# An infini-attention and FNet kernel whose planned order gets biases by kind of task and a jitter, drawn anew for each part of the plan

## The chip, the cores and the metric

The kernel runs on one core of one Trainium2 chip, as one program. The metric is the device time of one execution in microseconds. Before the change it is 1710.0 us, the median of three runs (1707.21 to 1713.73). The engines are called as in the profile: PE (TensorE), DVE (VectorE), ACT (ScalarE), POOL (GpSimd) and SP, which issues the DMAs. PEld is PE's loading of weights.

## The reference

Two layers, each of them an attention block with a compressive memory and then a Fourier mixing block, on 2048 rows of 512 numbers. Cut to what is computed:

```python
def A(x, wq, wk, wv, wo, beta):                 # 32 heads of 16, 4 segments of 512 rows
    q, k, v = heads(x @ wq), heads(x @ wk), heads(x @ wv)
    M, z = 0, 0
    for s in range(4):
        p = softmax(qs @ ks.T * scale + mask)   # inside the segment, causal
        a_mem = (phi(qs) @ M) / (phi(qs) @ z + 1e-6)
        o = g * a_mem + (1 - g) * (p @ vs)
        M, z = M + phi(ks).T @ vs, z + sum(phi(ks))
    return concat(o) @ wo

def B(x, seq_re, seq_im, hid_re, hid_im):
    a, b = x @ hid_re.T, x @ hid_im.T
    return seq_re @ a - seq_im @ b

for _ in range(2):
    x = x + A(layernorm(x), ...)
    x = x + B(layernorm(x), ...)
```

## The kernel before

Nearly all products are formed from pairs of float16 tiles: a number is split into a high and a low part, and three matmuls (high by high, high by low, low by high) add into one PSUM bank. Every tile that goes into such a product is therefore made by an ACT copy and a subtraction on DVE or POOL.

The work is cut into 32 attention groups (2 layers, 4 segments, 4 groups of 8 heads; the index `i`) and into Fourier units. Each kind of work is a Python generator in `body`:

- `s_p` and `s_v` project q, k and v (PE names `b<-g,w` and `b<-w,g`: `g` is the transposed layer-norm tile). `t_split` lays q and k out through DRAM into `qst` and `kst`.
- `s_x` multiplies q with k to find each row's maximum (`b<-kst,qst`, 62 rows of the array); `t_max` reduces each bank on DVE into `mx` (the custom instruction that writes `junk`). A transpose of `mx` on PE (`b<-identf,mx`) and a DMA put the maxima into two spare rows of `qst`.
- `s_st` forms the scores again, transposed and with the maximum taken off (`b<-qst,kst`, 64 rows); `t_sel` does exp on ACT and the causal mask on POOL (the affine selects).
- `s_av` multiplies with v (`b<-w,vt`, tiles of 128 by 32, four side by side); `s_m` and `t_merge` merge memory and attention; `s_o` is the output projection (`b<-wo,w`), after which `t_res` and `t_ln` add the residue and normalise.
- `s_c` turns the stored sequence matrix into float16 pairs, four tiles at a time: DVE maxima `cam`, a small matmul over the partitions (`b<-cam,ones`), a chain on DVE that gives the scale `csu`, ACT copies, and a subtraction.
- `s_ab` is the hidden transform of a row tile (`b<-wd,w`); `s_f` the sequence transform (`b<-w,w`, 128x512: 12 matmuls to a unit), each of whose units `t_y` adds into `y` on DVE.
- In the second layer the last two chunks of the sequence transform (`WIN` and up) are done with fewer multiplications: `t_sums` builds sums of matrix tiles on POOL and ACT, `t_six` sums of the hidden transform's results, and `t_win` multiplies them (`b<-w,w`, 128x256, 672 matmuls at the very end of the program).

The array is used in three tile shapes: whole (128 by 128), two halves of rows side by side (`mode="h"`: `s_x`, `s_st` and the read of the memory in `s_mem`), and four quarters of columns (`mode="v"`: `s_av`).

The order of all instructions is set when the program is built. `Plan` keeps a time for each engine, for each tile's last write and read, and for the slots of the shared SBUF and PSUM pools. A generator yields what its next step needs: engine, tiles read, pool slots, and the tile shape. The loop at lines 1391 to 1431 asks `Plan.ready` when each waiting step could start by the plan's clock, takes the larger of that and the time at which the step's engine is free, and then runs the first step in the list among those with the smallest time (lines 1426 and 1427, `SLACK` is 0). `Plan.turn` (line 67) adds `SWITCH`, 95 plan nanoseconds, where a PE step would change the tile shape, except that after `HOLD` = 700 nanoseconds in the whole shape it doesn't. `BESIDE` puts off a quarter step where a whole-shape step could start by then, and `TWICE` puts off the half steps of `s_x` and `s_st` until two of them fit, at most 1000 nanoseconds. Each engine runs its instructions in the order in which the loop wrote them; semaphores hold an instruction until its inputs are there. Every instruction is recorded by one helper (line 260), so all rows of the profile carry L260 and tiles are told apart by name: `w` is any slot of the shared SBUF pool, `b` any PSUM bank.

Of the kernel before, what the change touches and what calls it, by code (L numbers as in the profile page):

```python
# [2 lines left out]

# [29 lines left out]
BF16 = mybir.dt.bfloat16  # L33
NEG = -1e30
TICK = 10240 / 3
SLACK = 0
HOLD, SWITCH = 700.0, 95.0
TWICE, EARLY, BESIDE = 1000.0, 0.0, 1000.0
RESERVE = dict(G=500.0, Y=1000.0, V=0.0, A=0.0)
BATCH = 4  # L40
AGAIN = 0.0
FIRST = "cc", "craw"
NR = 3
K8192 = struct.unpack("<f", b"\x00\x70" * 2)[0]


class Plan:
# [4 lines left out]
    def __init__(self):  # L52
        self.free = dict.fromkeys("VGATYHD", 0.0)
        self.acc = {}
        self.cols = {}
        self.wr = {}
        self.rd = {}
        self.area, self.count, self.slot = {}, {}, {}
        self.fresh = set()
        self.port = dict(V=(0.0, 0.0), G=(0.0, 0.0))  # L60
        self.fine = {}
        self.by = {}
        self.late = False
        self.dma = None
        self.mode, self.units, self.begun, self.entered = "m", {}, 0.0, 0.0

    def turn(self, mode):

        now = self.free["T"]
        if mode == self.mode or self.mode == "m" and now - self.entered >= HOLD:  # L70
            return now
        return max(now, *self.units.values(), 0.0) + SWITCH

# [18 lines left out]
    def slots_free(self, kinds):  # L92
        extra, taken, r = {}, {}, 0.0
        for k in kinds:
# [8 lines left out]
            if n + len(busy) >= cap:  # L103
# [3 lines left out]
            keep = sum(max(0, lo - self.count[o] - extra.get(o, 0)) for o, (lo, _) in ar["kinds"].items()  # L107
                       if o != k and (n >= low or o in FIRST) and not (self.late and k == "ab" and o == "pt"))
            if k in ("ss", "sx") and n >= 4:
# [157 lines left out]
def body(ctx: ExitStack, tc: tile.TileContext, x, wq, wk, wv, wo, beta, wd, cs, out):  # L267
    nc = tc.nc
    pl = Plan()
    V, G, A, T, Y = (Eng(e, k, pl) for e, k in zip(  # L270
        (nc.vector, nc.gpsimd, nc.scalar, nc.tensor, nc.sync), "VGATY"))
# [46 lines left out]
    V.memset(mhalf, -0.5)  # L318
    kst = [const.tile([128, NP, 512], F16, name=f"kst{i}") for i in range(NR)]
    qst = [const.tile([128, NP, 512], F16, name=f"qst{i}") for i in range(NR)]  # L320
    vt = [const.tile([128, TT, NP, 3, 16], F32, name=f"vt{i}") for i in range(NR)]
    identf = const.tile([128, 128], F32, name="identf")
# [13 lines left out]
    def need(eng, *reads, tag=(), mode="m"):  # L336
        return eng, reads, (tag,) if isinstance(tag, str) else tag, mode
# [5 lines left out]
    def gate(*keys):  # L343
        return lambda: all(k in done for k in keys)
# [65 lines left out]
    used = set()  # L410

    def keep(n, g, w):
        yield gate(("dk", 0))
        yield need("Y", w)
        Y.dma_start(wqkv[g][n], w)
        yield lambda: (n, g) in used
        pl.close(w)

    def s_w():
        def part(n, g, how):  # L420
            i = 2 * g + n if n < 2 else 8
            yield need("A", tag="wv" if n == 2 else "wt")
            w = sb("wv" if n == 2 else "wt", F16, (128, 2, KT, 128))
            yield from how(w, stage[g][n], scl[:, i:i + 1])
            wnow[n, g] = w
            done.add(("W", n, g))
            if g < 2 and n < 2:
                spawn(keep(n, g, w))
            else:
                yield need("Y", w)  # L430
                Y.dma_start(wqkv[g][n], w)
# [77 lines left out]
    def s_k():  # L509
# [5 lines left out]

        for i in range(NR):
            for t, c in ((qst[i], 0.0), (kst[i], K8192)):
# [6 lines left out]
            if i == 0:  # L524
# [4 lines left out]
                yield gate(*[("L", 0, t) for t in range(TT)])  # L529
                for j in range(NR):  # L530
                    V.memset(vt[j][:, :, :, 1, :], 1.0)
# [119 lines left out]
    def t_split(p, key, f, kphi):  # L651
# [21 lines left out]
        i = key[1]  # L673
        if i >= NR:
            yield gate(("ST", i - NR))
# [160 lines left out]
    def s_psum():  # L836
        yield gate("WO")
        pl.floor("dft", 1)
        yield gate(("E", 3))
        kinds = pl.area["ss"]["kinds"]  # L840
        kinds["ss"], kinds["sx"] = (2, 6), (0, 6)

# [533 lines left out]
    def t_out(t, k):  # L1376
        yield gate(*[(*k, i) for i in range(6)])
        for i in range(2):
            yield need("Y", y)
            Y.dma_start(fins[1][t + i], y[:, t + i, :])  # L1380

    streams = [[None, s()] for s in (s_r, s_c, s_st, s_ln, s_w, s_x, s_mem, s_v, s_p, s_ab, s_f, s_wo, s_k, s_b, s_psum)]
    hots += [[None, s()] for s in (s_m, s_o, s_av,)]
    for s in hots + streams:
        s[0] = next(s[1])
    def settle(s):
        while callable(s[0]) and s[0]():
            s[0] = next(s[1], None)
        return s[0] is not None and not callable(s[0])

    while streams or hots or tasks or lows:
        best = None
        moved = True
        while moved:
            moved = False
            for s in hots + tasks + streams + lows:
                if callable(s[0]) and s[0]():
                    settle(s)
                    moved = True
        for group in (hots, tasks, lows):  # L1400
            group[:] = [s for s in group if s[0] is not None]
        streams[:] = [s for s in streams if s[0] is not None]
        ready, raw = [], {}
        for s in hots + tasks + streams + lows:
            w = s[0]
            if not callable(w):
                r = pl.ready(w[1], w[2], w[0])
                if r is not None:
                    free = pl.turn(w[3]) if w[0] == "T" else min(pl.free[e] for e in w[0])
                    ready.append((max(r, free), s))  # L1410
                    raw[id(s)] = r
        if pl.mode == "m":
            other = min((r for r, s in ready if s[0][0] == "T" and s[0][3] == "m"), default=1e18)
            for j, (r, s) in enumerate(ready):
                if s[0][0] == "T" and s[0][3] == "v" and r >= other:
                    ready[j] = max(r, raw[id(s)] + BESIDE), s
        if pl.mode != "h":
            other = min((r for r, s in ready if s[0][0] == "T" and s[0][3] != "h"), default=1e18)
            for j, (r, s) in enumerate(ready):
                w = s[0]  # L1420
                if w[2][:2] in (("ss", "ss"), ("sx", "sx")) and r + EARLY >= other:
                    both = pl.ready(w[1], w[2] + w[2][:2], w[0])
                    late = raw[id(s)] + TWICE
                    ready[j] = max(r, late if both is None else min(both, late)), s
        if ready:
            first = min(r for r, _ in ready)
            best = next(q for q in ready if q[0] <= first + SLACK)
        if best is None:
            assert not streams and not tasks, "stuck"
            break  # L1430
        best[1][0] = next(best[1][1], None)
# [45 lines left out]
```

## Time and profile before

| what | before |
|---|---|
| median of 3 runs | 1710.0 us |
| the profiled execution's own time | 1710.03 us |
| its span, first to last instruction | 1708.3 us |
| instructions | 33012 |
| DVE busy | 1174.4 us (69%) |
| ACT busy | 867.9 us (51%) |
| POOL busy | 848.4 us (50%) |
| mean granted TensorE clock | 0.987 |
| bytes moved by DMA | 228.16 MB |

A busy time is the union of an engine's instructions. Matmuls are pipelined, so a matmul's own duration is longer than the distance from its start to the next one's start; the rows of a timeline give both. A row of the view by windows gives, for a stretch of the span, each engine's busy time with its number of instructions, then the granted clock of TensorE, the share of time in which the DMA engines were busy, and GB/s.

### The profile page before, as it was taken

How to read it: one execution, taken by the hardware profiler on the slowest of the kernel's cores; microseconds unless marked ns; L12 is line 12 of the kernel's file. 1: busy time of each engine (PE TensorE's matmuls, PEld its weight loads, DVE VectorE, ACT ScalarE, POOL GpSimd, SP SyncE). 2: the span in 40 equal slices, each digit the busy share in tenths (PEclk: the TensorE clock that was granted, in tenths of full speed). 3: DMA queues.
4: the chain of work that ended last, by engine and by line, in shares of the span. 5: the costliest groups of instructions: out<-in, count | busy, mean ns of one | idle time of the engine just before them, and what ended most of it. 6: DMA issues, size and time to landing. Idle time of an engine off the chain costs nothing.

```text
span 1708.3 us, 33012 instructions
## 1 busy us (share of the span) xinstructions
PE 1640.5 (96%) x11324; PEld 765.1 (45%) x11324; DVE 1174.4 (69%) x3617; ACT 867.9 (51%) x1437; POOL 848.4 (50%) x1304
## 2 busy tenths in 40 slices
PE   5979999999999999999999999999999999999999
PEld 2424434344444443444444444444444443444488
DVE  6886776697968787455587776856777676442266
ACT  5558657628555556534446754454544444530341
POOL 6536647356544654443334654344643442570672
PEclk9979999999999999999999999999999999999999
DMA  8644635444654533344954764344544222416263
GB/s 207 163 137 119 177 106 158 131 124 127 171 148 127 167 106 100 117 111 154 248 150 161 209 171 117 76 114 133 131 109 116 76 75 63 131 25 197 86 185 118
DMA packets 221944, 228.16 MB, mean 134 GB/s; under 512 B 113232, under 2 KB 139856, under 8 KB 221776
## 3 DMA queue, kind: packets, MB, share of 16 engines
q1 hardware_dynamic: 221776, 226.06, 47.0%
q8 instruction: 89, 1.46, 0.4%
q14 instruction: 79, 0.65, 0.1%
HBM read 140.51 MB, written 61.87 MB: 118 GB/s over the span
## 4 chain that ended last, share of the span: by engine, by line
PE 77%; DVE 8%; issue 5%; ACT 4%; POOL 3%; DMA 2%; SPq 1%; ACTq 0%; POOLq 0%; DVEq 0%
PE b L260 77%; ACT w L260 4%; DVE junk L260 2%; POOL w L260 2%; DVE w L260 1%; SPq L260 1%; DVE y L260 1%; DMA w<-w 1%; DVE cam L260 1%; DMA w<-in_x_dram 0%; DVE mx L260 0%; DVE bst L260 0%; DMA w<-in_cs_dram 0%; DMA y<-in_wv_dram 0%; POOL rs L260 0%
## 5 line engine op out<-in xcount | busy, mean ns | idle before, releaser
L260 PEld LDWEIGHTS <-w 128*128 128x128 f16 x5280 | 493.8, 98 | 566.7 <-issue 88.2
L260 PE MATMUL b<-w,w 128*128 128x512 f16 (+1 forms) x3360 | 697.0, 359 | 6.7 <-ACT w L260 2.9
L260 POOL TENSOR_TENSOR w<-w,w 128x512 f16<-128x512 f32 (+3 forms) x364 | 403.9, 1120 | 304.0 <-ACT w L260 285.8
L260 ACT ACTIVATE w<-b,fac 128x512 f32<-128x512 f32 x664 | 409.6, 692 | 196.2 <-PE b L260 193.6
L260 DVE CUSTOM_DVE_ANT_0 junk<-b,cmask 128x256 bf16<-128x256 f32 (+3 forms) x1024 | 439.0, 483 | 61.2 <-PE b L260 59.9
L260 POOL TENSOR_SCALAR_AFFINE_SELECT w<-w 128x256 f32<-128x256 f32 (+1 forms) x640 | 228.9, 367 | 271.2 <-ACT w L260 266.5
L260 DVE SCALAR_TENSOR_TENSOR y<-b,fyu,y 128x512 f32<-128x512 f32 (+1 forms) x296 | 201.7, 686 | 179.5 <-PE b L260 179.1
L260 ACT ACTIVATE w<-w,csu 128x512 f16<-128x512 f32 x320 | 225.2, 720 | 106.2 <-POOL w L260 49.2
L260 ACT ACTIVATE w<-w 128x512 f16<-128x512 f32 (+2 forms) x160 | 98.3, 622 | 207.7 <-DVE w L260 161.7
L260 PE MATMUL b<-g,w 128*128 128x512 f16 x768 | 185.2, 383 | 7.0 <-DMA g<-w 4.9
L260 PE MATMUL b<-wd,w 128*128 128x512 f16 x768 | 181.1, 382 | 0.0
L260 PE MATMUL b<-w,vt 128*32 128x512 f32 (+3 forms) x2048 | 170.1, 451 | 1.4 <-POOL w L260 1.0
L260 DVE SCALAR_TENSOR_TENSOR w<-b,w 128x512 f16<-128x512 f32 x120 | 82.1, 684 | 108.6 <-ACT w L260 108.2
L260 ACT ACTIVATE w<-b 128x512 f16<-128x512 f32 (+1 forms) x128 | 76.4, 597 | 141.1 <-PE b L260 131.2
L260 PE MATMUL b<-kst,qst 62*128 62x256 f16 (+3 forms) x1024 | 124.3, 304 | 15.4 <-DVE mx L260 4.8
L260 POOL TENSOR_TENSOR w<-w,dn 128x256 f32<-128x256 f32 x109 | 67.5, 640 | 126.5 <-DVE dn L260 99.3
L260 PE MATMUL b<-qst,kst 64*128 64x512 f16 (+3 forms) x1024 | 115.5, 306 | 5.2 <-ACT w L260 2.9
L260 PE MATMUL b<-w,g 128*128 128x128 f16 x1536 | 97.1, 219 | 2.7 <-POOL w L260 1.8
L260 PEld LDWEIGHTS b<-w,vt 128*32 128x32 f32 x2048 | 57.9, 111 | 90.3 <-issue 62.1
L260 PEld LDWEIGHTS <-g 128*128 128x128 f16 x1536 | 87.6, 98 | 19.6 <-issue 14.7
L260 DVE STREAM_TRANSPOSE w<-b 128x512 f32<-128x512 f32 x112 | 73.6, 692 | 30.4 <-PE b L260 27.6
L260 PE MATMUL b<-wo,w 128*128 128x512 f16 x384 | 86.5, 379 | 0.1
(101 smaller groups left out, 1002.4 us busy)
## 6 DMA issues: line engine op xcount, KB each, us to landing
w<-in_cs_dram SPq DMA_DIRECT2D x160, 256.0 KB, 3.3
cc<-w SPq DMA_DIRECT2D x128, 256.0 KB, 2.8
w<-cc SPq DMA_DIRECT2D x112, 256.0 KB, 3.2
w<-w SPq DMA_DIRECT2D x96, 256.0 KB, 3.3
d<-w SPq DMA_DIRECT2D x128, 128.0 KB, 2.5
w<-in_x_dram SPq DMA_DIRECT2D x32, 256.0 KB, 3.7
qst<-d SPq DMA_DIRECT2D x64, 128.0 KB, 2.8
kst<-d SPq DMA_DIRECT2D x64, 128.0 KB, 2.9
```

Of the source, the lines that this page charges most:

```text
L260: r = f(*args, **kw)
```

## The change

The loop no longer takes the first of the steps with the smallest time. It takes the step with the smallest sum of that time and a bias. The plan is cut into parts of `SPAN` = 25000 plan nanoseconds of PE time, and each part has a number in `ORDER` (66 numbers, of which 43 are not zero; the last six are zero). A zero gives no bias and the old values. Another number seeds a generator of random numbers that draws, for that part: the most that a kind of task may be held back (0, 20, 60 or 200 ns; each generator function gets its own share of it), a jitter for each look at a step (up to 5, 20 or 60 ns), and values for `HOLD` (700, 1100 or 1500), `TWICE` (500, 1000 or 2000) and `BESIDE` (0, 1000 or 2500). No step is added or taken away; steps change places.

```diff
+SPAN = 25000.0
+ORDER = (
+    519897, 254532, 1662, 327161, 541694, 0, 608130, 0, 321687, 937175, 536548, 772191,
...
+    0, 0, 0, 0, 0, 0)
...
-        if mode == self.mode or self.mode == "m" and now - self.entered >= HOLD:
+        if mode == self.mode or self.mode == "m" and now - self.entered >= self.policy["HOLD"]:
...
+    def lean(k):
+        seed = ORDER[k] if k < len(ORDER) else 0
+        pol = pl.policy
+        pol.update(POLICY)
+        if not seed:
+            return lambda s: 0.0
+        rnd = random.Random(seed)
+        most, some = rnd.choice((0.0, 20.0, 60.0, 200.0)), rnd.choice((5.0, 20.0, 60.0))
+        pol["HOLD"] = rnd.choice((700.0, 700.0, 700.0, 1100.0, 1500.0))
+        pol["TWICE"] = rnd.choice((1000.0, 1000.0, 1000.0, 500.0, 2000.0))
+        pol["BESIDE"] = rnd.choice((1000.0, 1000.0, 1000.0, 0.0, 2500.0))
+        names = {}
+
+        def bias(s):
+            n = s[1].__name__
+            if n not in names:
+                names[n] = most * random.Random(f"{seed}{n}").random() ** 2
+            return names[n] + some * rnd.random()
+        return bias
...
     while streams or hots or tasks or lows:
         best = None
+        if pl.free["T"] >= SPAN * (part + 1):
+            part += 1
+            bias = lean(part)
...
-                    ready[j] = max(r, raw[id(s)] + BESIDE), s
+                    ready[j] = max(r, raw[id(s)] + pl.policy["BESIDE"]), s
...
-                    late = raw[id(s)] + TWICE
+                    late = raw[id(s)] + pl.policy["TWICE"]
...
-            first = min(r for r, _ in ready)
-            best = next(q for q in ready if q[0] <= first + SLACK)
+            best = min(ready, key=lambda q: q[0] + bias(q[1]))
```

The order of instructions on PE changes throughout. Three places are shown. In the rows below, the number after a name is the tile's number in that program, a row of LDWEIGHTS loads the weights of the matmul behind it, and the size is that of the result. The helper's line is 260 before and 269 now.

First, PE at the place where the transposed scores of attention group 8 begin (`b<-qst,kst` with `qst_109` and `kst_106`), while group 9 is still at its maxima (`b<-kst,qst` with `kst_104` and `qst_107`). Before:

```order
L260 LDWEIGHTS qst_107
L260 MATMUL b_5460<-kst_104,qst_107 128x384
L260 LDWEIGHTS qst_107
L260 MATMUL b_5461<-kst_104,qst_107 128x384
L260 LDWEIGHTS w_5363
L260 MATMUL b_5442<-w_4457,w_5363 128x512
L260 LDWEIGHTS w_5363
L260 MATMUL b_5442<-w_4457,w_5363 128x512
L260 LDWEIGHTS w_5363
L260 MATMUL b_5442<-w_4457,w_5363 128x512
L260 LDWEIGHTS kst_106
L260 MATMUL b_5477<-qst_109,kst_106 128x512
```

Now, at the same step of group 8:

```order
L269 LDWEIGHTS kst_106
L269 MATMUL b_5624<-qst_109,kst_106 128x512
L269 LDWEIGHTS kst_106
L269 MATMUL b_5625<-qst_109,kst_106 128x512
L269 LDWEIGHTS qst_107
L269 MATMUL b_5630<-kst_104,qst_107 128x128
L269 LDWEIGHTS qst_107
L269 MATMUL b_5631<-kst_104,qst_107 128x128
```

Before, three whole-shape matmuls of a Fourier unit stand between the two kinds of half steps; now the half steps follow each other. Counted over the whole of PE's order, the matmuls before fall into 859 stretches of one tile shape (369 whole, 389 halves, 101 quarters), and now into 747 (318, 332 and 97).

Second, PE where the scales of Fourier units 16 to 19 are summed over the partitions (the fifth `b<-cam,ones`). Before:

```order
L260 MATMUL b_4476<-identf,mx 32x128
L260 MATMUL b_4485<-cam,ones 128x4
L260 LDWEIGHTS w_4496
L260 MATMUL b_4519<-w_4057,w_4496 128x512
L260 LDWEIGHTS w_4496
L260 MATMUL b_4519<-w_4057,w_4496 128x512
L260 LDWEIGHTS w_4496
L260 MATMUL b_4519<-w_4057,w_4496 128x512
```

Now:

```order
L269 MATMUL b_4225<-cam,ones 128x4
L269 LDWEIGHTS w_3428
L269 MATMUL b_4199<-wd,w_3428 128x512
L269 LDWEIGHTS w_3428
L269 MATMUL b_4199<-wd,w_3428 128x512
L269 LDWEIGHTS w_3428
L269 MATMUL b_4199<-wd,w_3428 128x512
L269 MATMUL b_4240<-w_2467,macc 128x512
L269 MATMUL b_4241<-w_2467,macc 128x512
```

Before, the first matmul of unit 16 (`b_4519`) follows the small matmul at once. Now other work follows it: the hidden transform, a read of the memory, and another group's scores; unit 16 begins 97 rows further down.

Third, the end of the hidden transform (`b<-wd,w`) and the start of the last stage (128x256) on PE, now:

```order
L269 LDWEIGHTS w_20848
L269 MATMUL b_21100<-wd,w_20848 128x512
L269 LDWEIGHTS w_20625
L269 MATMUL b_20928<-w_19136,w_20625 128x512
L269 LDWEIGHTS w_20625
L269 MATMUL b_20928<-w_19136,w_20625 128x512
L269 LDWEIGHTS w_20625
L269 MATMUL b_20928<-w_19136,w_20625 128x512
L269 LDWEIGHTS w_20704
L269 MATMUL b_21144<-w_21014,w_20704 128x256
```

The same rows of `b<-wd,w` before:

```order
L260 LDWEIGHTS w_20414
L260 MATMUL b_20561<-wd,w_20414 128x512
L260 LDWEIGHTS w_20174
L260 MATMUL b_20536<-w_18292,w_20174 128x512
L260 LDWEIGHTS w_20174
L260 MATMUL b_20536<-w_18292,w_20174 128x512
```

Now the last hidden transform stands three matmuls ahead of the last stage; before, 776 rows stood between them. Counted in PE's order, 525 matmuls of plain Fourier units came after the last attention matmul before, and 81 come there now; 492 matmuls stood between the end of the hidden transform of the first of the two last chunks and the last stage, and 57 stand there now. The last stage itself has 672 matmuls in both. Ahead of the first `b<-wd,w` of the program stood 1006 matmuls, and 1050 stand there now. On POOL, 133 instructions stand behind the last affine select where 137 stood.

More of the change, by code (lines that the diff above doesn't have):

```diff
@@ L1 @@
+import random
 import struct
@@ L35 @@
 TICK = 10240 / 3
-SLACK = 0
-HOLD, SWITCH = 700.0, 95.0
-TWICE, EARLY, BESIDE = 1000.0, 0.0, 1000.0
+SWITCH, EARLY = 95.0, 0.0
+POLICY = dict(HOLD=700.0, TWICE=1000.0, BESIDE=1000.0)
 RESERVE = dict(G=500.0, Y=1000.0, V=0.0, A=0.0)
@@ L59, in __init__ @@
         self.fresh = set()
+        self.policy = dict(POLICY)
         self.port = dict(V=(0.0, 0.0), G=(0.0, 0.0))
@@ L412, in keep @@
     def keep(n, g, w):
-        yield gate(("dk", 0))
+        yield gate(("dk",0))
         yield need("Y", w)
@@ L838, in s_psum @@
         pl.floor("dft", 1)
-        yield gate(("E", 3))
+        yield gate(("E",3))
         kinds = pl.area["ss"]["kinds"]
@@ L1389, in settle @@
         return s[0] is not None and not callable(s[0])
+    def lean(k):
[16 more added lines that the diff above has]
+        return bias
+    part, bias = -1, None
     while streams or hots or tasks or lows:
         best = None
+        if pl.free["T"] >= SPAN * (part + 1):
+            part += 1
+            bias = lean(part)
         moved = True
```

4 rows, old and new, of the table ORDER are left out of this document.

## The prediction

> **What bounds the kernel now.** I read the head of the page first, then its slices, then the view by windows with stretches of my choice, and last the timeline of PE. The head gives the bound:
>
> ```profile
> span 1708.3 us, 33012 instructions
> PE 1640.5 (96%) x11324; PEld 765.1 (45%) x11324; DVE 1174.4 (69%) x3617; ACT 867.9 (51%) x1437; POOL 848.4 (50%) x1304
> PEclk9979999999999999999999999999999999999999
> ```
>
> PE is busy for 96% of the span and no other engine for more than 69%; it stands still for 1708.3 - 1640.5 = 67.8 us, and its granted clock dips in the first slices alone. The work on PE is the same after the change, so there are only three things an order can win: idle time, time at a low clock, and time that hides inside "busy". The windows say where the first two lie:
>
> ```profile
> 0.00:200.00 200.00, 157.41 (x1215) 72.87 (x1216) 157.89 (x582) 123.44 (x206) 116.33 (x188) 0.91 0.59 159
> 200.00:800.00 600.00, 588.78 (x3875) 259.54 (x3874) 429.12 (x1277) 339.54 (x559) 305.43 (x453) 0.99 0.46 132
> 800.00:1000.00 200.00, 190.41 (x1342) 91.86 (x1342) 149.99 (x464) 107.67 (x178) 93.26 (x131) 1.00 0.66 188
> 1000.00:1700.00 700.00, 699.41 (x4861) 337.07 (x4858) 433.36 (x1289) 297.25 (x498) 333.40 (x533) 1.00 0.40 112
> ```
>
> The first figure after the length is PE's busy time, the figure after POOL's count is the clock. PE idles 42.6 us in the first 200 us (and loses about 0.09 x 200 = 18 us to the clock), 11.2 us in the next 600 (about 6 us of clock), 9.6 us from 800 to 1000, and 0.6 us from 1000 to 1700. So outside the start there are some 27 us to be had. From 1000 us on PE is never without work; there only the third kind is left.
>
> **Changes of tile shape, the largest term.** This is what hides in "busy":
>
> ```profile
> 1000.39 1.47 PE L260 MATMUL b<-w,w 128*128 128x512 f16 x6
> 1001.79 0.39 PE L260 MATMUL b<-kst,qst 62*128 62x128 f16 x4
> 1002.12 1.47 PE L260 MATMUL b<-w,w 128*128 128x512 f16 x6
> ...
> 1005.24 0.61 PE L260 MATMUL b<-qst,kst 64*128 64x512 f16 x4
> 1005.78 1.04 PE L260 MATMUL b<-w,w 128*128 128x512 f16 x4
> ...
> 1010.02 2.12 PE L260 MATMUL b<-w,w 128*128 128x512 f16 x9
> ```
>
> Nine matmuls take 2.12 us and six 1.47, so three more cost 0.65, and one costs 0.217 us of PE. Six from 1000.39 should end their stream after 1.30 us, yet the half-shape step starts after 1.40: going in costs 0.10. Four half-shape matmuls of 128 columns, two side by side, are worth 2 x 0.217/4 = 0.11 and take 0.33: coming out costs 0.22. Four of 512 columns are worth 2 x 0.217 = 0.43 and take 0.54: coming out costs 0.11. One step in four is of the narrow kind (128 columns beside 256, 384 and 512), so a way out is (3 x 0.11 + 0.22)/4 = 0.14, and a change on the average (0.10 + 0.14)/2 = 0.12 us. The order has 859 stretches of one shape before and 747 now, thus 858 changes and 746: 112 fewer, worth 112 x 0.12 = **13.4 us**. Bounds: 11.2 us (all at 0.10) and 17.9 us (all at 0.16, the mean of 0.10 and 0.22). All of it lies on the path, since PE is the engine that sets the end, unless something else then comes late.
>
> A matmul's own length, with its way through the array, is in the page's groups:
>
> ```profile
> L260 PE MATMUL b<-wd,w 128*128 128x512 f16 x768 | 181.1, 382 | 0.0
> ```
>
> The Trainium skill, page "TensorEngine Tiling (Array Packing)", section "Key Properties", says that changing the tiling mode drains TensorE. By a full drain, taken as that length less the spacing (0.382 - 0.217), the term would be 112 x 0.165 = 18.5 us; the wide steps above cost 0.10 to 0.11, so the trace has less than that, and I keep 13.4.
>
> **The wait behind a scale, which goes.** Before, Fourier unit 16 follows its small matmul at once (second place shown with the change). The timeline there:
>
> ```profile
> 312.32 0.38 PE L260 MATMUL b<-cam,ones 128*128 128x4 f32 x2 [0.31 <-DVE cam L260]
> 315.20 0.87 PE L260 MATMUL b<-w,w 128*128 128x512 f16 x2 [2.50 <-ACT w L260]
> 317.19 1.03 PE L260 MATMUL b<-w,w 128*128 128x512 f16 x2 [1.11 <-POOL w L260]
> 300.00:325.00 25.00, 20.97 (x90) 7.44 (x89) 21.36 (x68) 13.18 (x24) 7.64 (x12) 0.86 0.27 71
> ```
>
> PE waits for the chain of DVE steps to the scale, for the ACT copy and for POOL's subtraction. From the small matmul's end (312.7) the second tile is there at 317.19, so 4.5 us of other work would cover it. Now 97 rows of other work stand between. The window shows 4.03 us idle and 0.14 x 25 = 3.5 us of clock: **7.5 us**. The lower bound is 3.6 us (the two gaps alone, if the clock falls elsewhere); it cannot be below nothing, since the unit comes later than its scale in any case.
>
> The Trainium skill, page "TensorE: Matmul & The Clock Gate", section "HAM oscillation — how this bites in real kernels", gives the rule that PE should have no idle gaps over about 3.4 us. By it the clock would have stayed up here, as no gap is over 2.50, and the term would be 4.0 us; the row has 0.86, so the trace decides, and short gaps close together count as well.
>
> **Filler that moves forward.** Before, 525 matmuls of plain Fourier units came after the last attention matmul, where PE never waits; now 81 do. The other 444 (444 x 0.217 = 96 us of PE work) stand between attention steps, in the second layer above all. That is cover for waits such as those from 800 to 1000, 9.6 us. I take half, **5 us**. Bounds: 9.6 us, if all are covered, and 5 us lost, for these 37 units bring their DVE sums along, into stretches where DVE is busy for 75% (149.99 of 200):
>
> ```profile
> L260 DVE SCALAR_TENSOR_TENSOR y<-b,fyu,y 128x512 f32<-128x512 f32 (+1 forms) x296 | 201.7, 686 | 179.5 <-PE b L260 179.1
> ```
>
> 37 x 0.686 is 25 us of DVE work; a fifth of it on the path is the 5 us.
>
> **What it costs: the end loses its cover.** The last stage needs the sums that POOL forms. This is POOL's work in before from the last affine select on:
>
> ```profile
> L260 POOL TENSOR_TENSOR w<-w,w 128x512 f16<-128x512 f32 x47 | 54.8, 1174 | 14.9 <-ACT w L260 14.4 <-POOL w L260 0.5
> L260 POOL TENSOR_TENSOR w<-w,w 128x256 f32<-128x256 f32 x50 | 37.1, 750 | 14.2 <-ACT w L260 12.1
> L260 POOL TENSOR_TENSOR w<-w 128x256 f32<-128x256 f32 x17 | 12.3, 728 | 7.0 <-DMA w<-in_cs_dram 4.0 <-ACT w L260 2.8
> 1650.00:1675.00 25.00, 25.00 (x231) 22.40 (x230) 17.94 (x32) 10.01 (x15) 19.69 (x24) 1.00 0.53 162
> ```
>
> These rows have 104.2 us; with the smaller groups it is 117 us. One 128x256 matmul costs 25/230 = 0.109 us, so behind the last attention matmul PE had 669 x 0.217 + 672 x 0.109 = 218 us of work; now it has 225 x 0.217 + 73 = 122 us. POOL's 117 us just fit, if POOL seldom stands still. Also the sums of the hidden transform's results, which must be ready when the last stage begins, had 492 matmuls (107 us) of room and now have 57 (12.4 us). In before that chain took from 1524.9, the end of the first row, to 1537.5, the end of the last:
>
> ```profile
> 1514.38 10.52 PE L260 MATMUL b<-wd,w 128*128 128x512 f16 x48
> 1523.09 9.06 POOL L260 TENSOR_TENSOR w<-w,w 128x256 f32<-128x256 f32 x9 [4.52 <-ACT w L260]
> 1536.32 1.16 POOL L260 TENSOR_TENSOR w<-w,w 128x512 f16<-128x512 f32 x1 [1.32 <-ACT w L260]
> ```
>
> That is 12.6 us, again about as long as the room. I put the loss at **6 us**; its bounds are nothing and 22 us (POOL at the share of 1650 to 1675, 19.69 of 25, needs 117/0.79 = 148 us, against 122 and the 4 us of attention matmuls that stand behind the last select).
>
> **The start** stays as it is: 0. There are 44 more matmuls (some 9.5 us) ahead of the first hidden transform, which may fill idle time; but they bring DVE work along, and DVE's 157.89 of 200 us is the load that PE waits for there. Bounds: 10 us won or lost.
>
> **The sum.** 13.4 + 7.5 + 5 - 6 = 19.9 us, so the span goes from 1708.3 to 1688.4. The profiled execution took 1710.03, 1.7 more than its span, and the median is 1710.0, so the forecast is 1688.4 + 1.7 = **1690 us**.
>
> **Rivals.** (1) Only the shape changes count: waits that go in one place come back in another, as the order on DVE and POOL has changed everywhere. 1710 - 13.4 = 1697. For it: those 112 are counted, all else is judged. (2) All waits after the start go, 11.2 + 9.6 + 0.6 + 6 = 27.4 us, and the end costs nothing: 1710 - 13.4 - 27.4 = 1669. For it: 96 us of filler is more than three times that. Against: filler helps only where the order puts it. (3) POOL becomes the bound of the end, with 16 us more than I took, at full clock: 1690 - 6 + 22 = 1706, which is no change: a measurement of this kernel tells about 0.5% (8.6 us) from none. (4) The same, with PE's clock falling as it waits, ends on the slow side. In the window at 300 us, 4.03 us idle became 7.5 lost, 1.86 times as much; 22 us become 41: 1690 - 6 + 41 = 1725. It decides from the point where the waits at the end take more than the 25.9 us that the rest wins, which at 1.86 are 14 us idle, that is POOL needing more than 140 us or being busy for less than 84% of that stage. Against (3) and (4): POOL's waits in the rows above are for ACT, at a time when nothing hurried it. That the change does nothing is out, by the counts.
>
> **How the numbers follow.** Forecast 0.46, (1) 0.19, (2) 0.13, (3) 0.13, (4) 0.09. Case (1) is still 0.8% faster. So faster by over 0.5%: 0.46 + 0.19 + 0.13 = 0.78, less 0.01 for (1) falling short, 0.77; within 0.5%: 0.14; slower by over 0.5%: 0.09. The bounds all at their best ends give 1710 - 17.9 - 7.5 - 9.6 - 10 = 1665, all at their worst 1710 - 11.2 - 3.6 + 5 + 22 + 10 = 1732; they will not all fall together. The range goes from (2), 1669, to (3), 1706, which leaves out (4) and the outer parts of (2) and (3).
>
> **What would show it.** Shape changes: 747 stretches, whose price can be read again; from 1000 us on the span must shrink although PE never waited there. The scale: a window around the fifth `b<-cam,ones` without an idle time over 1 us and a clock of 1.00. Filler: from 800 to 1000 us less than 5 us idle. The end: waits of `b<-w,w` 128x256 for POOL, together under 8 us, and POOL busy for over 90% after the last select. The prediction is wrong if the waits after 200 us have grown past 27 us, or if PE waits for POOL at the end for more than 14 us.

## The result and the profile after

The changed kernel takes 1668.67 us, the median of 4 runs (1668.08 to 1669.49), against 1710.84 us for the kernel before in 4 runs beside it (1707.21 to 1713.73). The ratio is 0.9755 with a 95% interval from 0.9735 to 0.9775. That is 42 us, twice the 20 us of the forecast, and 0.3 us below the low end of the range. The sign was right, and the time is that of rival (2), 1669 us, to which 0.13 had been given.

The head of the page of the changed kernel, with the clock's slices:

```profile
span 1667.8 us, 32731 instructions
PE 1620.1 (97%) x11324; PEld 772.2 (46%) x11324; DVE 1181.0 (71%) x3618; ACT 869.8 (52%) x1437; POOL 848.4 (51%) x1303
PEclk9788999999999999999999999999999999999999
```

The span is 40.5 us shorter: 20.4 us of PE's busy time have gone (1640.5 to 1620.1), though the matmuls are the same, and 20.1 us of its idle time (67.8 to 47.7). The view by windows, with the stretches that were shown of before, says where:

```profile
0.00:200.00 200.00, 162.03 (x1233) 78.81 (x1233) 159.60 (x592) 122.48 (x205) 117.12 (x187) 0.90 0.61 161
200.00:800.00 600.00, 597.12 (x3971) 269.06 (x3970) 447.11 (x1308) 355.29 (x580) 322.72 (x473) 1.00 0.48 141
800.00:1000.00 200.00, 197.07 (x1487) 95.77 (x1485) 146.98 (x477) 114.50 (x189) 98.22 (x150) 1.00 0.68 191
1000.00:1659.00 659.00, 658.84 (x4595) 324.27 (x4594) 422.90 (x1237) 277.55 (x465) 310.35 (x496) 1.00 0.39 110
```

The first 200 us are nearly as they were (PE idle for 38.0 us where it was 42.6, clock 0.90 where it was 0.91; by the clock intervals of the two traces PE ran at half clock there for 41.0 us where it was 34.1, so 3.4 us more are lost). From 200 to 800 the idle time fell from 11.2 to 2.9 us and the clock no longer dips; from 800 to 1000 idle time fell from 9.6 to 2.9 us. Later there is still none.

Two of the prediction's marks can be read at once. On the timeline of PE in the changed kernel, at the fifth `b<-cam,ones`:

```profile
290.23 0.61 PE L269 MATMUL b<-qst,kst 64*128 64x512 f16 x4
290.67 0.38 PE L269 MATMUL b<-kst,qst 62*128 62x128 f16 x4
291.06 0.38 PE L269 MATMUL b<-cam,ones 128*128 128x4 f32 x2
```

Four half-shape matmuls of 512 columns are worth 2 x 0.217 = 0.43 us, and the next kind of half step starts 0.44 us after the first: two half steps side by side pay nothing between them, which is one way in which the 112 changes of shape went. The window around it has no idle time and a full clock, where the same place before had cost 7.5 us:

```profile
275.00:300.00 25.00, 24.99 (x135) 11.27 (x133) 16.32 (x64) 16.57 (x27) 12.06 (x20) 1.00 0.39 127
```

And at the end, POOL's groups in the last 128 us of the changed kernel, and two of the windows there:

```profile
L269 POOL TENSOR_TENSOR w<-w,w 128x512 f16<-128x512 f32 x46 | 52.6, 1163 | 2.4 <-ACT w L269 2.4
L269 POOL TENSOR_TENSOR w<-w,w 128x256 f32<-128x256 f32 x53 | 39.7, 760 | 1.1
L269 POOL TENSOR_TENSOR w<-w 128x256 f32<-128x256 f32 x17 | 12.9, 769 | 0.0
```

```profile
1600.00:1625.00 25.00, 25.00 (x231) 22.40 (x229) 19.66 (x36) 13.36 (x23) 24.77 (x28) 1.00 0.77 233
1625.00:1650.00 25.00, 25.00 (x231) 22.42 (x229) 18.20 (x33) 13.04 (x21) 24.69 (x31) 1.00 0.45 157
```

POOL stands still for 3.5 us in all there (before 36 us in the three groups) and is busy for 99% of the two windows, and PE is busy for all of them. The stage fits, as the count of 117 against 122 us said it might.

### The profile page after: what moved, and what is told of

Read it like the earlier page. It is cut to its first block, busy times and chain, and to the rows that moved or that the text cites. A ratio compares the mean times of both kernels' runs of the same rounds, so it can differ in the third digit from the quotient of the medians.

```text
span 1667.8 us, 32731 instructions
## 1 busy us (share of the span) xinstructions
PE 1620.1 (97%) x11324; PEld 772.2 (46%) x11324; DVE 1181.0 (71%) x3618; ACT 869.8 (52%) x1437; POOL 848.4 (51%) x1303
## 4 chain that ended last, share of the span: by engine, by line
PE 85%; DVE 7%; ACT 3%; DMA 2%; issue 2%; POOL 1%; SPq 1%; ACTq 0%; DVEq 0%; POOLq 0%
PE b L269 85%; ACT w L269 2%; DVE junk L269 2%; DVE w L269 2%; DMA w<-w 1%; POOL w L269 1%; SPq L269 1%; DVE cam L269 1%; DVE y L269 0%; DMA w<-in_cs_dram 0%; DVE bst L269 0%; DMA y<-in_wv_dram 0%; DVE b L269 0%; DMA kst<-d 0%; DVE mx L269 0%
## 5 line engine op out<-in xcount | busy, mean ns | idle before, releaser
L269 POOL TENSOR_TENSOR w<-w,w 128x512 f16<-128x512 f32 (+2 forms) x363 | 403.1, 1123 | 208.9 <-ACT w L269 182.1
L269 PE MATMUL b<-wd,w 128*128 128x512 f16 x768 | 175.7, 379 | 0.0
L269 PEld LDWEIGHTS <-g 128*128 128x128 f16 x1536 | 90.2, 99 | 18.7 <-issue 11.2
```

The costliest lines, as they stand in the source:

```text
L269: r = f(*args, **kw)
```

## The experiments

Three theories stood against each other after the result. **Shapes**: the counted changes of shape are what is sure, and waits only move from place to place; this is what the forecast's largest term and rival (1) say. **Any draw**: holding kinds of task back and breaking ties loosens the order, whatever the numbers are. **Selected**: the numbers were picked so that the plan's own clock ends early, and that clock prices both the changes of shape and the waits of PE nearly as the chip does. The plan's clock on PE, read when the kernel is built, ends at 1676 us for before and at 1635 us for the changed kernel; the chip took 34 us more in both.

### e1: the same table with other numbers

```diff
-    519897, 254532, 1662, 327161, 541694, 0, 608130, 0, 321687, 937175, 536548, 772191,
+    519898, 254533, 1663, 327162, 541695, 0, 608131, 0, 321688, 937176, 536549, 772192,
...
```

> The changed kernel with every number of its table that is not zero raised by one, so that each part draws other biases and values. Its order has 779 changes of tile shape (before 858, changed kernel 746). Theory Shapes (the prediction's largest term decides, waits only move about): 79 fewer changes at 0.12 us, about 1701 us. Theory Any draw (holding kinds of task back and breaking ties loosens the order, whatever the numbers): near the changed kernel, about 1669. Theory Selected (the numbers were picked by the clock of the plan, which sees waits as well as changes of shape; plan's end plus 34 us holds for before, 1676 and 1710, and for the changed kernel, 1635 and 1669): the plan ends at 1727, so about 1761 us, slower than before.

Measured: 1755.69 us, ratio to before 1.0274 (1.0248 to 1.0300). 79 changes of shape fewer than before, and 48 us slower. Selected had 1761, 5 us too much; Shapes and Any draw fall. The windows and the waits of PE in this kernel:

```profile
200.00:800.00 600.00, 578.36 (x3834) 259.02 (x3833) 424.50 (x1274) 336.62 (x552) 301.45 (x458) 0.98 0.46 132
800.00:1000.00 200.00, 189.83 (x1192) 89.95 (x1193) 133.21 (x405) 91.92 (x150) 83.04 (x108) 0.97 0.57 158
1000.00:1700.00 700.00, 693.63 (x4733) 317.04 (x4732) 435.31 (x1313) 300.36 (x511) 316.85 (x526) 0.99 0.40 112
```

```profile
PE b L269 <- ACT w L269: 18.0, 36, 4.2
PE b L269 <- DMA w<-w: 4.6, 2, 4.0
PE b L269 <- DVE mx L269: 4.6, 10, 0.9
```

PE idles for 21.6, 10.2 and 6.4 us in the three windows, and loses some 25 us more to the clock (0.02 x 600 + 0.03 x 200 + 0.01 x 700). A bad draw costs what a good one wins, and it is paid in waits.

### e2 and e3: the first 8 and the first 40 numbers alone

The table is cut to `ORDER[:8]` and `ORDER[:40]`; parts without a number go by the old rule.

> Only the first 8 of the 66 numbers are kept, the rest are zero: the order is biased in the first 200 us alone and as before by rule from there on. 825 changes of shape. Theory Shapes: 33 fewer, about 1707 us. Theory Any draw: 6 of 43 drawn parts, about 1705. Theory Selected: the plan ends at 1656, so about 1690 us; the waits after 200 us, which no number of this table touches directly, must then be well below before's 27 us, since the first 200 us give only some 4.

> Only the first 40 of the 66 numbers are kept. 796 changes of shape. Theory Shapes: 62 fewer, about 1703 us. Theory Any draw: 1685. Theory Selected: the plan ends at 1640.5, so about 1674.5 us.

Measured: 1689.30 us (0.9888, from 0.9871 to 0.9904) and 1677.00 us (0.9813, from 0.9795 to 0.9831). Selected had 1690 and 1674.5. With the first 8 numbers alone, which touch the order up to 200 us, the windows are:

```profile
200.00:800.00 600.00, 591.91 (x3928) 263.91 (x3928) 435.63 (x1291) 348.35 (x573) 318.71 (x471) 1.00 0.48 138
800.00:1000.00 200.00, 195.74 (x1441) 93.26 (x1439) 151.77 (x505) 115.52 (x191) 98.44 (x150) 1.00 0.65 182
```

The idle time from 200 to 1000 us is 8.1 + 4.3 = 12.4 us, where before had 20.8, in a stretch whose rules are those of before. The first numbers give the rest of the plan another state to start from. The numbers from 8 to 39 bring another 12 us. In this kernel 531 matmuls of plain Fourier units still stand behind the last attention matmul (525 before): the filler has not moved, and two fifths of the waits have gone all the same.

### e4: biases without the drawn policies

```diff
-        pol["HOLD"] = rnd.choice((700.0, 700.0, 700.0, 1100.0, 1500.0))
-        pol["TWICE"] = rnd.choice((1000.0, 1000.0, 1000.0, 500.0, 2000.0))
-        pol["BESIDE"] = rnd.choice((1000.0, 1000.0, 1000.0, 0.0, 2500.0))
+        drawn = {}
+        drawn["HOLD"] = rnd.choice((700.0, 700.0, 700.0, 1100.0, 1500.0))
+        drawn["TWICE"] = rnd.choice((1000.0, 1000.0, 1000.0, 500.0, 2000.0))
+        drawn["BESIDE"] = rnd.choice((1000.0, 1000.0, 1000.0, 0.0, 2500.0))
```

> The numbers of the changed kernel, with the drawn biases and jitter, but HOLD, TWICE and BESIDE stay at their old values. 784 changes of shape, 74 fewer than before. Theory Shapes: about 1702 us. Theory Any draw (the biases do it): 1669 to 1690. Theory Selected: numbers that were picked for another course of the plan are worth nothing here; the plan ends at 1757, so about 1791 us, with the loss in idle time of PE and not in changes of shape.

Measured: 1795.00 us, ratio 1.0505 (1.0485 to 1.0525), with 74 changes of shape fewer than before; Selected had 1791. The windows:

```profile
200.00:800.00 600.00, 561.43 (x3640) 242.13 (x3640) 407.00 (x1213) 322.77 (x530) 282.00 (x429) 0.97 0.45 128
1000.00:1700.00 700.00, 679.71 (x4598) 303.80 (x4596) 429.24 (x1329) 295.01 (x501) 303.53 (x516) 0.99 0.38 108
```

PE idles for 38.6 us from 200 to 800 and 20.3 us from 1000 to 1700, where even before had 0.6. This does not say that the biases are harmful: a number is worth something only in the plan for which it was picked, and this is another plan. Which of the knobs carries the gain can't be told in this way and stays open.

### e5 and e6: the price of a change of shape

Ahead of the first product into two of the three banks of each last-stage unit, six matmuls into the part of the bank that nothing reads; e6 has the first of each pair in the whole shape as well:

```diff
+    def touch(o):
+        for r in range(3):
+            T.matmul(o[:, 256:], kst[0][0:64, 0, 0:128], qst[0][0:64, 0, 0:256], start=True, stop=True, skip_group_check=True)
+            T.matmul(o[:, 256:], kst[0][:, 0, 0:128], qst[0][:, 0, 0:256], start=True, stop=True, skip_group_check=True)
...
         px = ps("dft")
+        touch(px)
...
         py = ps("dft")
+        touch(py)
```

> The changed kernel with 192 extra matmuls of 256 columns in the last stage, where PE never waits: ahead of two of the three first products of each of its 16 units, three times a half-shape matmul (64 rows) and a whole-shape one, into a part of the bank that nothing reads. 938 changes of tile shape in place of 746. To be read against e6_shape_whole, which has the same matmuls all in the whole shape. Theory Shapes cost 0.11 us each (the median over a change in the traces, wide steps): 192 x 0.11 = 21 us more than e6. The prediction's 0.12: 23 us more. A full drain of 0.165: 32 us more. Theory Hidden (the price lies beside other work): no more than e6.

> As e5_shape_half, but the 96 half-shape matmuls use all 128 rows, so that no change of tile shape is added (746). 192 matmuls of 256 columns at 0.109 us: 21 us more than the changed kernel's 1669, about 1690, by every theory, if PE alone is the bound of the last stage; less, if PE would have waited there.

Measured: 1708.96 us for e5 and 1688.73 us for e6. The whole-shape matmuls cost what their columns cost, 20.1 us; the 192 changes cost 20.2 us more, 0.105 us each. On the timeline of e5:

```profile
1620.48 1.35 PE L269 MATMUL b<-qst,kst 64*128 64x256 f16 x6
1621.67 3.44 PE L269 MATMUL b<-w,w 128*128 128x256 f16 x30
1625.04 1.35 PE L269 MATMUL b<-qst,kst 64*128 64x256 f16 x6
```

From 1620.48 to 1621.67 are 1.19 us for six matmuls worth 0.65, with five changes between the first of them and the next row: 0.107 each. So the price is real and lies on the path. These are changes between the whole shape and single half steps only. The price of the changes that the kernels really have can be read from the starts of the matmuls in the traces of before and of the changed kernel: the time from the start of one stretch of a shape to the start of the next, less what its columns are worth, its idle time and the low clock. From 200 us to the last stage that is 96.0 us at 769 changes before and 82.2 us at 663 now, 0.125 and 0.124 each (short waits inside the half and quarter stretches are in it): some 0.10 out of the whole shape, 0.13 to 0.14 from halves back to the whole shape, and 0.15 to 0.18 out of quarters. The forecast's 0.12 was right, and the changes that went there were worth 13.8 us.

### e7 and e8: more work for POOL at the end

```diff
         ttw(d[:, lo], b[:, lo], b[:, hi], OP.add)
+        ttw(d[:, lo], b[:, lo], b[:, hi], OP.add)
+        ttw(d[:, lo], b[:, lo], b[:, hi], OP.add)
```

> The changed kernel with the first POOL step of each of the 16 sums of the last stage done three times over (the same result): 32 more POOL instructions of 0.75 us, 24 us, behind the last attention group. Theory Cover lost (the prediction's term for the end was wrong in size alone: POOL now just fits and has little room left): PE waits in the last stage, 12 to 20 us more than the changed kernel, about 1685. Theory Room left (POOL had far more room than the count of 117 against 122 us says): within 3 us of 1669.

> The kernel before with the same 32 additional POOL instructions. Both theories: there POOL has some 100 us of room behind the last attention matmul, so no change, within 3 us of before.

Measured: 1689.07 us for e7, on the changed kernel, 20.4 us more than it; 1708.15 us for e8, on the kernel before, ratio 1.0006 (0.9994 to 1.0018). Some 24 us of POOL work cost nothing where 525 matmuls of filler lay behind the attention, and 20 us where 78 do (the planner counts the added steps, so the order of e7 differs a little from that of the changed kernel). The last windows of e7:

```profile
1625.00:1650.00 25.00, 15.80 (x109) 11.71 (x108) 14.59 (x22) 10.97 (x19) 24.45 (x29) 0.80 0.22 72
1650.00:1675.00 25.00, 18.57 (x168) 15.92 (x167) 13.08 (x25) 10.03 (x15) 24.14 (x30) 1.00 0.43 149
```

```profile
L269 PE MATMUL b<-w,w 128*128 128x256 f16 x672 | 77.7, 278 | 15.6 <-POOL w L269 10.1 <-ACT w L269 3.4 <-DVE w L269 2.1
```

POOL is busy throughout, PE waits for it, and the clock falls to 0.80 in a window with 9.2 us idle. So the danger that the prediction named is there; the changed kernel has about 4 us of room left (24 less 20.4, an estimate).

### e9 and e10: numbers of my own

For each part in turn, the one of 24 (e9) or 44 (e10) random numbers, or zero, with which the plan's clock ends first; no run on a chip went into it.

> The first 8 numbers of the changed kernel, and behind them numbers of my own (10 that are not zero among 29, the rest zero): for each part in turn the one of 24 random numbers, or zero, with which the plan's clock ends first. 821 changes of tile shape. Theory Shapes: 37 fewer than before at 0.11, about 1704 us. Theory Selected: the plan ends PE at 1642.5, so about 1676 us, with the gain in waits. Theory Any draw: 16 of 43 drawn parts, about 1693.

> The first 40 numbers of the changed kernel and then my own, 10 of them not zero, found in the same way among 44 for each part. 745 changes of shape; the plan ends PE at 1635.1, as it does for the changed kernel. Theory Selected: the same time as the changed kernel within 4 us, about 1669. Theory These very numbers (what the table has was found by runs on a chip, so that other numbers with an equal plan do worse): 1675 (as e3) or more.

Measured: 1676.08 us (0.9811, from 0.9795 to 0.9828) and 1669.45 us (0.9771, from 0.9756 to 0.9785). Both are what the plan's end plus 34 us says, to half a microsecond. e9's windows:

```profile
200.00:800.00 600.00, 596.01 (x3953) 264.97 (x3953) 445.59 (x1298) 350.71 (x574) 321.21 (x472) 1.00 0.50 141
800.00:1000.00 200.00, 198.27 (x1470) 94.86 (x1469) 152.47 (x505) 114.52 (x189) 94.28 (x146) 1.00 0.67 188
```

And those of e10:

```profile
200.00:800.00 600.00, 597.25 (x3972) 268.61 (x3971) 447.15 (x1306) 355.40 (x580) 323.63 (x474) 1.00 0.48 142
800.00:1000.00 200.00, 196.59 (x1486) 95.84 (x1485) 147.50 (x479) 113.96 (x189) 97.70 (x149) 1.00 0.69 192
```

e9 idles for 4.0 + 1.7 = 5.7 us from 200 to 1000, the same as the changed kernel's 5.8, with 498 plain Fourier matmuls behind the last attention matmul and 821 changes of shape. All kernels side by side; the fifth column is PE's idle time from 200 to 1000 us, the last the plain Fourier matmuls behind the last attention matmul:

| kernel | changes of shape | plan's end of PE, us | time, us | idle, us | filler behind |
|---|---|---|---|---|---|
| before | 858 | 1676.2 | 1710.8 | 20.8 | 525 |
| changed | 746 | 1635.1 | 1668.7 | 5.8 | 81 |
| e1 | 779 | 1727.4 | 1755.7 | 31.8 | 141 |
| e2 | 825 | 1655.7 | 1689.3 | 12.4 | 531 |
| e3 | 796 | 1640.5 | 1677.0 | 5.3 | 417 |
| e4 | 784 | 1757.1 | 1795.0 | 52.3 | 249 |
| e9 | 821 | 1642.5 | 1676.1 | 5.7 | 498 |
| e10 | 745 | 1635.1 | 1669.5 | 6.2 | 363 |

Time less the plan's end lies between 28 and 38 us in all eight. The idle time follows neither the changes of shape nor the filler; it grows with the plan's end. e10 has another end than the changed kernel (POOL's last instruction ends at 1635.9 us of its trace, where the changed kernel's ends at 1656.9), and the same time. No version was faster than the changed kernel beyond its interval.

## Why the prediction was off

**Changes of shape: right.** 112 at 0.12 us were to give 13.4. Behind the first 200 us the traces show 0.125 each, 13.8 us for the 106 that went there; e5 against e6, with one kind of change, shows 0.105 and that all of it lies on the path.

**The wait behind a scale: right.** The window at its place has full clock and no idle time; 7.5 us won.

**Filler that moves forward: the step that failed.** The prediction put 5 us on it, "cover for waits such as those from 800 to 1000", and judged everything else that waits to stay as it is. Measured, the idle time and clock after the start fell from 11.2 + 5.1 + 9.6 + 0.6 = 26.5 us to 2.9 + 0 + 2.9 + 0.2 = 6.0, so 20.5 us were won where this term and the scale together had 12.5. (The 5.1 us are half of the 10.2 us that the trace of before shows at half clock from 200 to 800 us; the prediction's 6 came from a rounded 0.99.) And the cause was wrong, not the size alone: with the filler left at the end (531 and 498), e2 loses 8.4 of the 20.8 us of idle time from 200 to 1000 us, and e9 loses 15.1; and e1 has more of it than before, with the filler moved (141). What the idle time does go with is the plan's own clock, for the order as a whole. When the kernels are built, PE stands still in that clock behind its first 200 us (in gaps over 0.15 us) for 25.5 us before, for 4.1 us after the change, and for 45.0 us in e1. How the numbers of the table were found isn't on record; e9 and e10 show that picking by this clock alone is enough. The prediction read two places of the order and took the rest as unchanged; the stretch from 200 to 800 alone gave 13.4 us, of which the scale had 7.5.

**The end: the danger was right, its price was not.** This is the second step that failed. 6 us were put down for POOL; PE never waited there. POOL ran at 99%, not at the 79% which had set the bound: its waits in before were idle time of an engine that nobody hurried. e7 and e8 show that the cover is gone, and that the room is some 4 us.

**The start: nearly right.** 0 was forecast; 4.6 us of idle time went, less 3.4 us of clock. (The kernels as built have 1038 and 1090 matmuls ahead of the first hidden transform, so 52 more and not 44; the term was put at 0 either way.)

**The sum.** 13.4 + 7.5 + 5 - 6 = 19.9 us were forecast for the span. Shapes 13.8, waits behind the start 20.5, the start 1.2 and the end 0 give 35.5 of the 40.5 us measured. The other 5.0 us lie in PE's busy time. By the same reading of matmul starts, 2.2 of them went at the changes of shape in the first 200 us, where short waits are in the same figure, and 1.6 between whole-shape matmuls; the rest was not taken apart. Rival (2) had both failing steps nearly right, at 13.4 + 27.4 = 40.8 us. That it meets the measured time so closely is in part luck: 6.0 us of its waits stayed, and the start and the short waits, which it had at nothing, made up for them.

## What to carry to other kernels

Where a planner writes the order, an edit to its rule can't be judged by the few places that one reads: count what can be counted over the whole order, and give the unread rest a range as wide as all the waits that it could remove or add. Random choices inside such a planner are worth nothing by themselves in the two orders tried here whose numbers had not been picked for them (e1 and e4 are 3 and 5% slower than before). They pay through selection, by a clock whose differences hold on the chip (to within 10 us over the eight orders, from 28 to 38), and whoever changes a rule or a constant of the planner has to pick the numbers anew. Idle time of an engine in a stage where it was not hurried says little on how fast it can go when it is (POOL went from 79% to 99%): add the busy times and compare the sum with the room.

## What the runs showed of the hardware

A change between whole-shape and half-shape matmuls costs 0.105 us on average over 192 of them, and a change of any kind 0.124 us over the 663 of the changed kernel from 200 us on; both are less than the 0.165 us by which a matmul's length exceeds its spacing (0.382 less 0.217). Two half steps of different tiles next to each other cost nothing between them (0.44 us from start to start for 0.43 us of columns). TensorE's granted clock fell to 0.80 in a 25 us window of e7 and to 0.86 in one of before, with 9.2 and 4.0 us of idle time in several pieces, of which the longest were 2.9 and 2.5 us. In these traces the clock is either full or half, and a stretch at half clock inside the program is a multiple of 3.41 us long: the 0.86 is 6.8 us at half clock, the 0.80 is 10.2.
